# Second layer of a two-layer mixture: second-product matmuls issued in turn with first-product matmuls, and large tiles moved to one address phase

## The chip, the core and the metric

One core of one Trainium2 chip. The metric is the device time of one execution in microseconds, here the median of three runs.

## What is computed

Attention with a local window and some global keys over q, k, v (2 x 8 heads x 768 x 64) gives x, 1536 tokens by 512. A first layer follows, then a second layer of eight experts with a gate that is normalised over rows and columns in turn:

```python
x = x @ w_in                      # 512 -> 2048
g = h * (1.0 / (1.0 + np.exp(-h)))
x = g @ w_out                     # 2048 -> 512
...
for e in range(E):                # 8 experts
    h = np.maximum(x @ w1[e], 0.0)        # 512 -> 1024
    ye = h @ w2[e]                        # 1024 -> 512
    out += P[:, e:e + 1] * ye
```

All inputs and the output are float32.

## The kernel before, in words

Every float32 operand of a matmul is split into a high and a low part of the type that TensorE takes at full speed; a product is three matmuls (high by high, high by low, low by high) that add up in PSUM.

The program has three stages. Attention runs interleaved with the first layer (`step`, `emit_h`, `emit_y`), and the second layer (`layer2`) comes last. The change is in the second layer, and by the addresses of its tiles it touches the others.

The second layer works through 48 units. Unit u is one expert's half of the hidden columns (512 of 1024; 16 of these, counted by q) and one block of 512 tokens (tb, three of them). In a unit the first product x @ w1 is 512 x 512 x 512. It is made as seven products of 256-blocks with sums and differences of blocks (a fast 2 x 2 scheme, line 326 for the weights): `h_product(u, i)`, with i in 0, 5, 4, 6, 3, 1, 2 in this order. Each is 12 matmuls of 128 x 256, with the split weights `wc[i]` as the stationary and the split tokens `xc[tb][i]` as the moving operand. The results stand in PSUM banks: 0 and then 1 add up in the one bank "h", 5 and 6 in one of three banks "a", 4 and 2 in another, 3 in the third. DVE sums them (`h_sum`, lines 410, 476, 480), ACT applies the Relu and makes the high part (line 402), DVE the low part (line 403, `h_split`). The hidden values go into one of five pairs of tiles, room_hh / room_hl (three pairs), room_g and roomh / rooml.

The second product h @ w2 of a unit is made one unit later. `y_part(u - 1, k)`, k = 0..3, takes 128 hidden columns and issues 12 matmuls of 128 x 512: for each of four token tiles i three matmuls into bank `y[i]`, with hidden values as the stationary and w2 rows as the moving operand. After k = 3 the four banks are added to the output, weighted by the gate (`y_add`, line 440).

`window(u)` writes this order down by hand: product 0, 5, part 0, product 4, part 1, products 6 and 3, part 2, product 1, part 3, product 2. Parts are whole blocks of 12 matmuls, and so are products. A scheduler that looks at priorities then places each engine's instructions, so some move a little. In windows where new weights are due, `w_combine(i)` after a product and `w_split(k)` after a part make the next split weights with ACT and POOL (lines 342, 343).

Tiles lie in pools that grow from the left of a partition (xp, hid, wf, ring and the constants) and in pools on its right (the late one, gp, with wc0 to wc2, roomh, rooml and the tokens xc of the first two blocks). In the names of rows, xc_0xh, xc_1xh, xc_0xl and xc_1xl are the tokens of the third block, which lie on the left, plain xc those of the first two, on the right. wx0 and wx1 are weights on the left. Small tiles at the head of the pools set where the large ones begin: those on the left at 32 bytes past a multiple of 256, those on the right at 96 past.

Of the kernel before, what the change touches and what calls it, by code (L numbers as in the profile page):

```python
# [8 lines left out]
F32 = mybir.dt.float32  # L9
# [11 lines left out]
P = 128  # L21
# [16 lines left out]
HB = TB // 2  # L38
ORDER = 0, 5, 4, 6, 3, 1, 2
TINY = 1.125 * 2.0**-15  # L40

# [5 lines left out]
class Kernel:  # L47
# [29 lines left out]
    def setup(self, const, pre):  # L77
        nc = self.nc
# [28 lines left out]
        nc.vector.scalar_tensor_tensor(flag, self.ng, float(G), fl[:, 1:2], op0=ALU.is_le, op1=ALU.mult)  # L107
        self.flag = flag
        for _ in self.att_turn(0, const):
            pass  # L110
# [262 lines left out]
    def h_product(self, u, i):  # L373

        nc = self.nc
# [8 lines left out]
        for f in range(2):  # L384
            fs = slice(f * P, (f + 1) * P)
            for k in range(2):
                for a, b in ((ah, bh), (ah, bl), (al, bh)):
# [4 lines left out]
                    n += 1  # L392
        return ps

# [18 lines left out]
    def y_part(self, u, k, tiles=range(4)):  # L413
# [4 lines left out]
        for i in tiles:  # L418
# [3 lines left out]
            for j, (a, b) in enumerate(((hh, wh), (hh, wl), (hl, wh))):  # L422
                nc.tensor.matmul(  # L423
                    self.y[i], a, b, start=k == 0 and j == 0, stop=k == 3 and j == 2, skip_group_check=True
                )

    def y_add(self, u, i):
# [18 lines left out]
    def window(self, u, side):  # L446

        nc, n_units = self.nc, self.E * self.NH * self.NB
        q, tb = divmod(u, self.NB)
        y = iter(range(4)) if u else iter(())  # L450

# [3 lines left out]

        def second():
            k = next(y, None)
            if k is not None:
                self.y_part(u - 1, k)
                if u % self.NB == 0:  # L460
                    self.w_split((2, 3, 0, 1)[k])

        def first(i):
            ps = self.h_product(u, i)
            if more:
                self.w_combine(i)
            next(side, None)
            return ps

# [4 lines left out]
        b2 = first(5)  # L474
        second()
        nc.vector.tensor_tensor(u2, s1, b2, op=ALU.add)  # L476
        b3 = first(4)
        second()
        first(6)
        nc.vector.tensor_tensor(u3, s1, b2, op=ALU.add)  # L480
        b4 = first(3)
        hq[1, 1] = self.h_sum(u3, b3, ALU.add)
        hq[1, 0] = self.h_sum(u3, b4, ALU.subtract)
        second()
        first(1)
        hq[0, 0] = self.h_split(b1)
        second()
        if u:
# [11 lines left out]
    def layer2(self):  # L500
# [4 lines left out]
        for i in range(4):  # L505
            for k in range(4):
                self.y_part(n_units - 1, k, (i,))
            self.y_add(n_units - 1, i)
# [455 lines left out]
    def rest(self):  # L964

        yield from self.x_combine(self.NB - 1)
# [183 lines left out]
```

## Time and profile before

| | |
|---|---|
| runs | 1441.61, 1444.14, 1444.32 us, median 1444.14 |
| profiled execution | 1444.39 us |
| its span, first to last instruction | 1442.6 us |
| mean granted TensorE clock | 0.989 |
| TensorE matmuls busy | 1413.3 us (98% of the span), 8552 |
| weight loads busy | 1232.1 us (85%) |
| VectorE (DVE), ScalarE (ACT), GpSimd (POOL) busy | 739.9, 487.2, 553.6 us |

The busy time of TensorE is the time in which at least one matmul is recorded. Matmuls overlap in the records, so the mean duration of one (280 ns for 256 columns) is longer than the time from one start to the next. The chain that ended last follows the work back from the end: where an engine waited for nobody, it goes to the instruction before on the same engine.

### The profile page before, as it was taken

The numbers are of one execution on the slowest core, as the hardware profiler recorded it, in microseconds if no ns is written. First come the engines' busy times: TensorE is split into PE (matmuls) and PEld (weight loads), VectorE is DVE, ScalarE is ACT, GpSimd is POOL, SyncE is SP. The second block draws the span as 40 slices with busy tenths as digits, with TensorE's granted clock in tenths as the row PEclk, the third lists the DMA queues.
The fourth block names the chain that finished last, engine by engine and source line by source line (L and its number), as shares of the span: only waits on it lengthen the run. The fifth ranks groups of instructions, "written<-read, shape, count | busy, mean of one in ns | idle before, by whom it ended". The sixth has DMA issues, their size and how long they took to land.

```text
span 1442.6 us, 21250 instructions
## 1 busy us (share of the span) xinstructions
PE 1413.3 (98%) x8552; PEld 1232.1 (85%) x8552; DVE 739.9 (51%) x1298; ACT 487.2 (34%) x949; POOL 553.6 (38%) x489
## 2 busy tenths in 40 slices
PE   8998999999999999999999999999999999999998
PEld 6776687778888989999998999899899899989997
DVE  8899545456353556544354354435444443544443
ACT  6665545555352422222232221223222132322220
POOL 5677755444470423314142331414224141422210
PEclk8899999999999999999999999999999999999999
DMA  9685442222230201011010101102010110201001
GB/s 257 178 245 186 154 121 73 74 74 88 88 103 1 59 1 59 16 44 41 19 50 10 59 16 44 44 16 57 3 59 22 38 45 15 59 0 45 1 28 63
DMA packets 75292, 92.18 MB, mean 64 GB/s; under 512 B 30640, under 2 KB 49072, under 8 KB 75184
## 3 DMA queue, kind: packets, MB, share of 16 engines
q1 hardware_dynamic: 72880, 82.34, 19.2%
q10 hardware_dynamic: 2304, 8.39, 1.5%
q8 instruction: 69, 1.13, 0.3%
q14 instruction: 39, 0.32, 0.1%
HBM read 79.19 MB, written 11.53 MB: 63 GB/s over the span
## 4 chain that ended last, share of the span: by engine, by line
PE 89%; DVE 8%; issue 1%; ACT 1%; POOL 0%; DMA 0%; DVEq 0%; ACTq 0%; SPq 0%; POOLq 0%
PE y L423 37%; PE h L388 32%; PE y L276 7%; PE h L237 3%; PE h L238 3%; PE h L239 3%; PE a_s L726 2%; DVE wf L201 1%; DVE wf L203 1%; DVE wf L199 1%; DVE wf L205 1%; PE a_o L783 1%; PE a_f L764 1%; DVE s L735 1%; DVE st L744 0%
## 5 line engine op out<-in xcount | busy, mean ns | idle before, releaser
L480 DVE TENSOR_TENSOR tabs<-tabs,h 128x512 f32<-128x512 f32 x48 | 33.0, 687 | 333.9 <-PE h L388 333.9
L343 POOL TENSOR_TENSOR wc0l<-wf,wc0h 128x512 fp32r<-128x512 f32 x16 | 21.2, 1323 | 340.3 <-ACT wc0h L342 340.3
L440 DVE SCALAR_TENSOR_TENSOR x<-y,gate,x 128x512 f32<-128x512 f32 x168 | 115.5, 742 | 18.3 <-PE y L423 18.3
L343 POOL TENSOR_TENSOR wx1l<-wf,wx1h 128x512 fp32r<-128x512 f32 x64 | 89.9, 1405 | 79.7 <-ACT wx1h L342 79.5
L402 ACT ACTIVATE room_hh<-tabs 128x512 fp32r<-128x512 f32 x87 | 54.2, 629 | 190.9 <-DVE tabs L410 188.5
L410 DVE TENSOR_TENSOR tabs<-tabs,h 128x512 f32<-128x512 f32 x144 | 98.8, 687 | 19.0 <-PE h L388 16.8
L343 POOL TENSOR_TENSOR wx0l<-wf,wx0h 128x512 fp32r<-128x512 f32 x48 | 62.1, 1293 | 90.3 <-ACT wx0h L342 90.3
L388 PE MATMUL h<-xc,wx1h 128*128 128x256 f32 x512 | 93.4, 280 | 1.7 <-DVE tabs L410 1.7
L388 PE MATMUL h<-xc,wx0h 128*128 128x256 f32 x512 | 93.4, 280 | 0.6 <-DVE tabs L476 0.6
L423 PE MATMUL y<-wx1h,room_hh 128*128 128x512 f32 x232 | 91.2, 393 | 0.0
L423 PE MATMUL y<-wx0h,room_hh 128*128 128x512 f32 x232 | 91.2, 393 | 0.0
L423 PE MATMUL y<-wx0l,room_hh 128*128 128x512 f32 x232 | 90.8, 391 | 0.0
L423 PE MATMUL y<-wx1l,room_hh 128*128 128x512 f32 x232 | 90.8, 391 | 0.0
L423 PE MATMUL y<-wx0h,room_hl 128*128 128x512 f32 x232 | 90.7, 391 | 0.0
L423 PE MATMUL y<-wx1h,room_hl 128*128 128x512 f32 x232 | 90.7, 391 | 0.0
L403 DVE SCALAR_TENSOR_TENSOR room_hl<-tabs,room_hh 128x512 fp32r<-128x512 f32 x87 | 77.6, 898 | 25.5 <-ACT room_hh L402 24.2
L342 ACT ACTIVATE wx1h<-wf 128x512 fp32r<-128x512 f32 x64 | 40.4, 632 | 141.8 <-PE y L423 84.2
L388 PEld LDWEIGHTS h<-xc,wx0h 128*128 128x128 f32 x512 | 82.6, 188 | 5.8 <-DVE tabs L476 0.8
L221 POOL TENSOR_TENSOR w1l<-wf,w1h 128x512 fp32r<-128x512 f32 x48 | 67.0, 1395 | 50.9 <-ACT w1h L220 44.6
L388 PEld LDWEIGHTS h<-xc,wx1h 128*128 128x128 f32 x512 | 80.4, 188 | 4.4 <-DVE tabs L410 1.9
L221 POOL TENSOR_TENSOR w0l<-wf,w0h 128x512 fp32r<-128x512 f32 x48 | 67.0, 1397 | 42.0 <-ACT w0h L220 40.2
L276 PE MATMUL y<-hh,w1h 128*128 128x512 f32 (+1 forms) x208 | 83.0, 399 | 0.0
(270 smaller groups left out, 4143.3 us busy)
## 6 DMA issues: line engine op xcount, KB each, us to landing
wf<-in_moe_w_dram SPq DMA_DIRECT2D x64, 512.0 KB, 3.7
wf<-w SPq DMA_DIRECT2D x32, 512.0 KB, 3.3
ra<-in_moe_w_in_dram SPq DMA_DIRECT2D x16, 512.0 KB, 6.0
rb<-in_moe_w_out_dram SPq DMA_DIRECT2D x16, 512.0 KB, 5.3
w<-wf ACTq DMA_DIRECT2D x16, 512.0 KB, 4.3
vw<-in_v_dram SPq DMA_DIRECT2D x8, 448.0 KB, 4.5
qr<-in_q_dram SPq DMA_DIRECT2D x12, 256.0 KB, 5.8
kr<-in_k_dram SPq DMA_DIRECT2D x12, 256.0 KB, 6.0
```

Source lines behind the costliest of these rows:

```text
L221: nc.gpsimd.tensor_tensor(lo, src, f32(hi), op=ALU.subtract)
L237: nc.tensor.matmul(ps, ah, bh, start=i == 0, stop=False)
L238: nc.tensor.matmul(ps, ah, bl, start=False, stop=False)
L239: nc.tensor.matmul(ps, al, bh, start=False, stop=i == last)
L276: nc.tensor.matmul(self.y[i][:, cols], a, b, start=begin and j == 0, stop=f == self.NF1 - 1 and j == 2, skip_group_check=True,)
L343: self.nc.gpsimd.tensor_tensor(dst[1], src, f32(dst[0]), op=ALU.subtract)
L388: nc.tensor.matmul(ps[:, f * HB:(f + 1) * HB], a[:, k, fs], b[:, k, :], start=first and n == 0, stop=n == 11, skip_group_check=True,)
L402: self.nc.scalar.activation(hi, src, AF.Relu)
L403: self.nc.vector.scalar_tensor_tensor(lo, src, 0.0, f32(hi), op0=ALU.max, op1=ALU.subtract)
L410: self.nc.vector.tensor_tensor(c, a, b, op=op)
L423: nc.tensor.matmul(self.y[i], a, b, start=k == 0 and j == 0, stop=k == 3 and j == 2, skip_group_check=True)
L440: nc.vector.scalar_tensor_tensor(acc, self.y[i], self.gate[:, t, e:e + 1], acc, op0=ALU.mult, op1=ALU.add)
```

## The change

In `window`, parts are no longer called as blocks. `h_product` and `y_part` became generators that give way after each matmul, and `first(i, k)` issues one matmul of product i, then one of part k, twelve times. Product 4 goes with part 0, 6 with part 1, 3 with part 2, 1 with part 3; products 0, 5 and 2 stand alone. The last unit's parts, after the loop, stay blocks. Two pads that nothing reads are allocated: 224 bytes at the head of the left side (in `setup`) and 96 bytes on the right (in `rest`). With them every large tile that a matmul of the two layers reads begins at a multiple of 256 bytes.

```diff
+PAD_L, PAD_R = 224, 96
...
         self.flag = flag
+
+        const.tile([P, PAD_L // 4], F32, tag="pad", name="pad")
...
     def h_product(self, u, i):
...
                     n += 1
-        return ps
+                    yield
...
     def y_part(self, u, k, tiles=range(4)):
...
+                yield
...
-        y = iter(range(4)) if u else iter(())
...
-        def second():
-            k = next(y, None)
-            if k is not None:
-                self.y_part(u - 1, k)
-                if u % self.NB == 0:
-                    self.w_split((2, 3, 0, 1)[k])
-
-        def first(i):
-            ps = self.h_product(u, i)
+        def first(i, k=None):
+
+            second = self.y_part(u - 1, k) if u and k is not None else iter(())
+            for _ in self.h_product(u, i):
+                next(second, None)
+            if u and k is not None and tb == 0:
+                self.w_split((2, 3, 0, 1)[k])
             if more:
                 self.w_combine(i)
             next(side, None)
-            return ps
+            return self.hb[{0: 0, 1: 0, 5: 1, 6: 1, 4: 2, 2: 2, 3: 3}[i]]
...
         b2 = first(5)
-        second()
         nc.vector.tensor_tensor(u2, s1, b2, op=ALU.add)
-        b3 = first(4)
-        second()
-        first(6)
+        b3 = first(4, 0)
+        first(6, 1)
         nc.vector.tensor_tensor(u3, s1, b2, op=ALU.add)
-        b4 = first(3)
+        b4 = first(3, 2)
         hq[1, 1] = self.h_sum(u3, b3, ALU.add)
         hq[1, 0] = self.h_sum(u3, b4, ALU.subtract)
-        second()
-        first(1)
+        first(1, 3)
         hq[0, 0] = self.h_split(b1)
-        second()
...
     def rest(self):
-
+        self.gp.tile([P, PAD_R // 4], F32, tag="pad", name="pad")
```

What the scheduler makes of it, on TensorE where product 4 of unit 25 meets part 0 of unit 24. Before (names: h_25_4 is the bank of that product, y_24_3 that of token tile 3):

```order
L423 MATMUL y_24_2_8621<-wx0h_4209,room_hl_4218 128x512
L423 MATMUL y_24_3_8625<-wx0h_4209,room_hh_4215 128x512
L423 MATMUL y_24_3_8625<-wx0l_4210,room_hh_4215 128x512
L423 MATMUL y_24_3_8625<-wx0h_4209,room_hl_4218 128x512
L388 MATMUL h_25_4_8630<-xc_4_3710,wc2h 128x256
L388 MATMUL h_25_4_8630<-xc_11_3717,wc2h 128x256
L388 MATMUL h_25_4_8630<-xc_4_3710,wc2l 128x256
```

The whole part stands ahead of the whole product. In the changed program, the head of the same product, with the last rows of product 5 before it:

```order
L391 MATMUL h_25_5_8602<-xc_12_3719,wc1h 128x256
L391 MATMUL h_25_5_8602<-xc_5_3712,wc1l 128x256
L391 MATMUL h_25_4_8616<-xc_4_3711,wc2h 128x256
L426 MATMUL y_24_0_8618<-wx0h_4210,room_g_4220 128x512
L391 MATMUL h_25_4_8616<-xc_11_3718,wc2h 128x256
L426 MATMUL y_24_0_8618<-wx0l_4211,room_g_4220 128x512
L391 MATMUL h_25_4_8616<-xc_4_3711,wc2l 128x256
L426 MATMUL y_24_0_8618<-wx0h_4210,room_g_4221 128x512
```

Each matmul of the product is now followed by one of the part.

The second place is TensorE at the head of a window, unit 25 after product 2 of unit 24. Before:

```order
L388 MATMUL h_24_4_8466<-xc_9_3447,wx1h_4203 128x256
L388 MATMUL h_24_4_8466<-xc_2_3440,wx1l_4204 128x256
L388 MATMUL h_25_0_8586<-xc_0_3706,wc0h 128x256
L388 MATMUL h_25_0_8586<-xc_7_3713,wc0h 128x256
L388 MATMUL h_25_0_8586<-xc_0_3706,wc0l 128x256
```

In the changed program:

```order
L391 MATMUL h_24_4_8450<-xc_9_3448,wx1h_4204 128x256
L391 MATMUL h_24_4_8450<-xc_2_3441,wx1l_4205 128x256
L391 MATMUL h_25_5_8602<-xc_5_3712,wc1h 128x256
L391 MATMUL h_25_5_8602<-xc_12_3719,wc1h 128x256
L391 MATMUL h_25_0_8588<-xc_0_3707,wc0h 128x256
L391 MATMUL h_25_0_8588<-xc_7_3714,wc0h 128x256
```

Two matmuls of product 5 now stand ahead of product 0, the one that writes bank "h".

The third place is DVE at the end of window 22. Before (x_0 is the output of a token block, y_21_0 to y_21_3 the four banks of the second product, h_22_0 the bank "h", h_22_4 the bank of products 4 and 2):

```order
L403 SCALAR_TENSOR_TENSOR room_hl_4217<-h_22_0_8078,room_hh_4214 128x512
L440 SCALAR_TENSOR_TENSOR x_0_2317<-y_21_0_8105,gate,x_0_2317 128x512
L440 SCALAR_TENSOR_TENSOR x_0_2317<-y_21_1_8109,gate,x_0_2317 128x512
L440 SCALAR_TENSOR_TENSOR x_0_2317<-y_21_2_8113,gate,x_0_2317 128x512
L440 SCALAR_TENSOR_TENSOR x_0_2317<-y_21_3_8117,gate,x_0_2317 128x512
L410 TENSOR_TENSOR tabs<-tabs,h_22_4_8122 128x512
```

In the changed program:

```order
L444 SCALAR_TENSOR_TENSOR x_0_2318<-y_21_0_8110,gate,x_0_2318 128x512
L406 SCALAR_TENSOR_TENSOR room_hl_4217<-tabs,room_hh_4214 128x512
L444 SCALAR_TENSOR_TENSOR x_0_2318<-y_21_1_8117,gate,x_0_2318 128x512
L444 SCALAR_TENSOR_TENSOR x_0_2318<-y_21_2_8124,gate,x_0_2318 128x512
L444 SCALAR_TENSOR_TENSOR x_0_2318<-y_21_3_8131,gate,x_0_2318 128x512
L406 SCALAR_TENSOR_TENSOR room_hl_4218<-h_22_0_8080,room_hh_4215 128x512
L413 TENSOR_TENSOR tabs<-tabs,h_22_4_8108 128x512
```

The read of bank "h" (line 403, now 406) moved from ahead of the four additions to behind them. (Lines 388, 402, 403, 410, 423 and 440 of the kernel before are 391, 405, 406, 413, 426 and 444 of the changed one.)

## Rows read from the trace of the kernel before

**Rows 1.** The page, parts 1 and 4: busy time, and the chain by engine.
```profile
PE 1413.3 (98%) x8552; PEld 1232.1 (85%) x8552; DVE 739.9 (51%) x1298; ACT 487.2 (34%) x949; POOL 553.6 (38%) x489
...
PE 89%; DVE 8%; issue 1%; ACT 1%; POOL 0%; DMA 0%; DVEq 0%; ACTq 0%; SPq 0%; POOLq 0%
```

**Rows 2.** Second layer: PE, PEld, DVE, ACT, POOL busy (count), clock, DMA share, GB/s.
```profile
420.90:1437.20 1016.30, 1013.03 (x6377) 913.68 (x6375) 475.33 (x704) 255.80 (x427) 302.43 (x227) 1.00 0.11 34
```

**Rows 3.** The same stretch, line 388 alone and line 423 alone: PE, PEld, clock, DMA.
```profile
420.90:1437.20 1016.30, 509.32 (x4032) 503.67 (x4031) 1.00 0.11 34
...
420.90:1437.20 1016.30, 561.98 (x2304) 419.77 (x2304) 1.00 0.11 34
```

**Rows 4.** Chain of waits, one window: start us, length us, what.
```profile
941.97 4.29 PE h L388 x36
946.25 2.75 PE y L423 x12
949.00 1.43 PE h L388 x12
950.43 2.75 PE y L423 x12
953.18 2.83 PE h L388 x24
956.01 2.79 PE y L423 x12
958.80 1.42 PE h L388 x12
960.22 2.78 PE y L423 x12
```

**Rows 5.** TensorE's timeline, four stretches, first and last row: start, length, what.
```profile
902.82 0.28 PE L388 MATMUL h<-xc_0xl,wc1l 128*128 128x256 f32 x1
...
903.95 0.40 PE L423 MATMUL y<-wx0h,room_hh 128*128 128x512 f32 x1
...
911.05 0.28 PE L388 MATMUL h<-xc_1xl,wx0h 128*128 128x256 f32 x1
...
912.37 0.28 PE L388 MATMUL h<-xc_0xh,wx1h 128*128 128x256 f32 x1
...
1020.27 0.39 PE L423 MATMUL y<-wx0h,room_hh 128*128 128x512 f32 x1
...
1021.63 0.40 PE L388 MATMUL h<-xc,wx0h 128*128 128x256 f32 x2
...
1010.43 0.40 PE L423 MATMUL y<-wx0h,roomh 128*128 128x512 f32 x1
...
1011.84 0.40 PE L388 MATMUL h<-xc,wc2h 128*128 128x256 f32 x2
```

**Rows 6.** The end: chain piece of the last 48 y; timeline of the last matmul and addition.
```profile
1426.12 11.06 PE y L423 x48
...
1436.77 0.40 PE L423 MATMUL y<-wx1h,room_hl 128*128 128x512 f32 x1
1437.20 0.75 DVE L440 SCALAR_TENSOR_TENSOR x<-y,gate,x 128x512 f32<-128x512 f32 x1 [2.04 <-PE y L423]
```

**Rows 7.** Weight loads (page; tile lg: ns min/median/max), and lg's matmuls in the timeline.
```profile
L388 PEld LDWEIGHTS h<-xc,wx0h 128*128 128x128 f32 x512 | 82.6, 188 | 5.8 <-DVE tabs L476 0.8
...
L534 PEld LDWEIGHTS lg<-xc,wg x40: 93/94/96, 344.1 to 373.8; 128*16 128x16 f32 x40
...
344.34 1.88 PE L534 MATMUL lg<-xc,wg 128*16 128x256 f32 x15
```

**Rows 8.** DVE's timeline after product 1 of one window: start, length, what.
```profile
1023.93 0.69 DVE L403 SCALAR_TENSOR_TENSOR room_hl<-h,room_hh 128x512 fp32r<-128x512 f32 x1 [2.71 <-ACT room_hh L402]
1024.54 2.71 DVE L440 SCALAR_TENSOR_TENSOR x<-y,gate,x 128x512 f32<-128x512 f32 x4
```

**Rows 9.** Groups of the page: line 403 where it reads SBUF.
```profile
L403 DVE SCALAR_TENSOR_TENSOR room_hl<-tabs,room_hh 128x512 fp32r<-128x512 f32 x87 | 77.6, 898 | 25.5 <-ACT room_hh L402 24.2
```

More of the change, by code (lines that the diff above doesn't have):

```diff
@@ L446, in window @@
     def window(self, u, side):
-        nc, n_units = self.nc, self.E * self.NH * self.NB
+        nc = self.nc
         q, tb = divmod(u, self.NB)
-        y = iter(range(4)) if u else iter(())
         more = tb == self.NB - 1 and q + 1 < self.E * self.NH
@@ L506, in layer2 @@
             for k in range(4):
-                self.y_part(n_units - 1, k, (i,))
+                for _ in self.y_part(n_units - 1, k, (i,)):
+                    pass
             self.y_add(n_units - 1, i)
```

## The prediction

> **What bounds the kernel now.** I read the page first, then the busy time of the last stage, then the chain of waits inside it, then single steps of TensorE in the timeline. The page gives TensorE 1413.3 us of matmuls in a span of 1442.6 us, and the chain that ended last is 89% TensorE [rows 1]. The change lives in the second layer, from 420.9 to 1437.2 us: 1016.3 us at a granted clock of 1.00, that is 2.4 GHz, with TensorE busy for 1013.0 of them, so idle for 3.3 [rows 2]. There line 388 issues all 4032 matmuls of the first products ("h", 256 columns) and line 423 all 2304 of the second ("y", 512 columns) [rows 3]. The stage is a stream of matmuls, and its length is their number times the time from one start to the next, which I call a step. Busy times don't give steps, because records overlap; the chain does, since it counts each matmul from the end of the one before. One whole window there holds 9.97 us of 84 h (118.7 ns) and 11.07 us of 48 y (230.6 ns) [rows 4]. Check: 4032 x 118.7 + 2304 x 230.6 = 478.6 + 531.3 = 1009.9 us, with the idle time within 3 us of the stage.
>
> At 2.4 GHz 256 columns are 106.7 ns and 512 are 213.3 ns, so each h carries 12.0 ns and each y 17.3 ns that are not columns: 48.4 + 39.9 = 88 us in all. Only these 88 us, and new waits, can move. They aren't constant. Ten steps of 128x256 with xc_0xl and wc1 took 1.13 us (113 ns), eleven with xc_0xl and wx0 took 1.32 us (120 ns); six y with room_hh and room_hl took 1.36 us (226.7 ns), six with roomh and rooml 1.41 us (235 ns) [rows 5]. Shape, clock and neighbours are alike, so the difference must come from where the tiles lie. As the program is laid out, tiles of the left side begin 32 bytes past a multiple of 256, those of the right side 96 past.
>
> **The change, term by term.**
>
> *Taking turns.* No matmul is added or removed. Products 4, 6, 3 and 1 of 47 units are issued one h, one y, 12 + 12. If a step depended on its neighbour's kind, blocks of different length would show it. Blocks of 12 h take 1.42 and 1.43 us, of 24 2.83, of 36 4.29: 118 to 119 ns whatever the length; blocks of 12 y take 2.75 to 2.79, which is 229 to 233 ns, and the last 48 in one piece 11.06, which is 230.4 [rows 4, 6]. So I take 0. A block of 12 could hide 5 ns per change of kind from me, so the bounds are 96 x 47 changes x 5 ns, 22 us either way.
> One might expect more because of the weight load: one of 128 columns is recorded with 188 ns, one of 16 columns with 94 [rows 7], so 128 columns cost some 107 ns, as long as an h streams, and a y gives it twice that time. But 15 matmuls of 256 columns with those 16-column loads still take 14 steps in 1.88 - 0.28 us, 114 ns each [rows 7]. A shorter load barely shortens the step; a longer cover for the load shouldn't either.
>
> *One phase.* The pads of 224 and 96 bytes bring every large tile to a multiple of 256. The trace never shows that place: every operand of these two lines begins 32 bytes past a multiple of 64. Bounds: at the best all 88 us go; at the worst every step becomes the dearest seen, 120 and 235 ns, +5.2 +10.1 = +15 us. The rows point both ways. For h equal places are dear (xc_0xl with wx0, both at 32: 120) and unequal ones cheap (xc_0xl at 32 with wc1 at 96: 113); for y equal ones are cheap (226.7) and unequal ones, roomh and rooml at 96, dear (235) [rows 5]. What speaks for a gain is the ratio of the cheap steps: 113/106.7 and 226.7/213.3 are both 17/16. One column's time is added for every 16 columns, that is for every 64 bytes streamed, which is what a stream would pay whose pieces of 64 bytes each straddle a boundary. With that removed the steps should at least come down to the cheap ones. I take the nearest rows: 114 ns for h (113 to 114 [rows 5, 7]) and 228 for y, a little over 226.7 since most y now stand between two h: (118.7 - 114) x 4032 = 19.0 us and (230.6 - 228) x 2304 = 6.0 us, together -25.0 us.
> The Trainium skill ("TensorE: Matmul & The Clock Gate", Part 2, step 1) says that TensorE reads the moving operand and the weights through two independent ports, so that loading weights takes nothing from a running matmul. By it no placing of weights against moving tiles could matter, and this term would be 0; rows 5 show 113 against 120 ns, so here the measurement decides against it.
>
> *A new wait.* Product 0 of the next unit writes the one bank "h" that product 1 of this unit fills, so it waits until ACT and DVE have read it (lines 402 and 403). Before, a block of 12 y stood between, 2.8 us of slack. Now DVE makes the four additions of line 440 first, as the order of the change shows. The last addition starts 0.43 us after the last y starts, 0.03 after that y's record ends [rows 6]; the next instruction of DVE follows 0.68 us later (four in 2.71) and takes 0.69 [rows 8]. So the bank is free 1.80 us after that y starts, and 0.03 more for the signal. TensorE meanwhile has that y, 12 h of product 2 and 2 of product 5, which the scheduler put in front: 0.23 + 14 x 0.1187 = 1.89 us, or 1.83 with h at 114 ns. Nothing to spare, and nothing waited if all is on time. Line 403 has a mean of 898 ns where it reads SBUF [rows 9], against 0.69 us where it reads the bank; were DVE late by that 0.21 us every time, 46 windows would cost 9.7 us. Between 0 and 9.7 I take 3 us, nearer to on time.
>
> *What costs nothing.* Splitting the next weights (lines 342, 343) is issued at the end of the same products; ACT and POOL are busy for 255.8 and 302.4 us of the stage's 1016.3 [rows 2], and the queue of DMA issues is in the same order. If that cover went, product 5 of the next unit would wait for its weights. The four additions need to free their banks before product 4 of the next unit, 36 h or 4.2 us after the last y, and are done in 1.1.
>
> **The sum.** The profiled execution took 1444.39 us, 0.25 us above the median of 1444.14. 1444.4 + 0 - 25.0 + 3 = 1422.4, say **1422 us**.
>
> **The rivals.** A difference under 0.2% (2.9 us) can't be told from none here; all chances use that bound.
>
> 1. *Neither part does anything.* The steps stay as they are, and the wait stays near 0 to 3: **1446 us** at the middle. For: blocks of every length have the same step. Against: steps do depend on place. Chance 0.18.
>
> 2. *Slower: equal places are the dear case for h.* The weight load and the stream hit the same part of SBUF together, as xc_0xl with wx0 does. 4032 x (120 - 118.7) = +5.2 us, y at 229.5 -2.5, the wait +3 to +9.7: **1450 to 1457 us**. It decides as soon as h steps stand above 118.7 ns. For: the equal-place rows of h [rows 5]. Against: those were also off the 64-byte grid, and no row shows them on it. Chance 0.30.
>
> 3. *The whole extra column per 16 goes.* Steps of 109 and 217 ns: (118.7 - 109) x 4032 + (230.6 - 217) x 2304 = 39.1 + 31.3 = 70 us less, the wait grows to 5: **1379 us**, and something less again if the first layer's matmuls gain alike. For: the ratio 17/16. Against: nothing in the trace runs at such a step, and the extra may be the chip's own. Chance 0.12.
> The Trainium skill (same page, "Back-to-back issue gap") gives N/2.4 + 2.5 ns for a warm stream, 109 and 216 ns; by it the result would be an estimate of some 1377 us. No step of this trace is that short.
>
> **How the numbers follow.** Forecast 0.40, rivals 0.18, 0.30 and 0.12. The forecast spreads over 1405 to 1439 as h lands between 111 and 117 ns. Faster: 0.40 + 0.12 = 0.52; same 0.18; slower 0.30. A range of 80% leaves out most of rival 3 and the upper end of rival 2: 1390 to 1455 us.
>
> **What would show it.** Right: in the chain, 12 h plus 12 y in 4.10 us or less (4.18 to 4.22 now as two blocks), blocks of h alone at 114 ns, and under 0.1 us of idle before product 0 in each window. Rival 1: all blocks as now. Rival 2: h alone at 120 and the pair at 4.2 or more. Rival 3: pairs at 3.95. The forecast is wrong if blocks of h still show 118 ns or more, or if TensorE's waits on DVE exceed 10 us.

## The result, and the profile after

The changed kernel takes **1460.82 us** (median of 4 runs, 1458.88 to 1462.03) against 1444.16 (four runs of the kernel before): 1.0115 times as long, 95% interval 1.0102 to 1.0129, so 16.7 us slower. The forecast was 1422 with a range of 1390 to 1455: the sign is wrong, and the time lies above the range. The profiled execution took 1458.88 us with a span of 1457.1.

The page, parts 1 and 4, the lines that answer to [rows 1]:

```profile
PE 1429.9 (98%) x8552; PEld 1237.0 (85%) x8552; DVE 735.2 (50%) x1298; ACT 488.0 (33%) x949; POOL 546.1 (37%) x489
...
PE 89%; DVE 7%; POOL 1%; ACT 1%; issue 1%; DMA 0%; ACTq 0%; SPq 0%; DVEq 0%; POOLq 0%
```

TensorE has the same 8552 matmuls and is busy 16.6 us longer. Its weight loads grew by 4.8 us and ACT by 0.8; DVE and POOL are busy for less time than before. The second layer alone, whole and then by its two matmul lines (h is now line 391, y line 426), the columns of [rows 2, 3]:

```profile
418.90:1452.00 1033.10, 1029.83 (x6377) 919.28 (x6375) 472.83 (x705) 256.88 (x426) 293.38 (x227) 1.00 0.11 33
...
418.90:1452.00 1033.10, 851.93 (x4032) 644.53 (x4031) 1.00 0.11 33
...
418.90:1452.00 1033.10, 810.05 (x2304) 432.92 (x2304) 1.00 0.11 33
```

The layer went from 1016.3 us [rows 2] to 1033.1, at the same granted clock of 1.00, and TensorE is idle for 3.3 us in both. So the loss is in the steps of one stream; a short wait shows there as a longer step and not as idle time, since the records overlap. (The busy times of the two lines overlap each other here and can't be added.) The chain of waits shows one unit of work:

```profile
905.00 0.23 PE y L426
905.23 4.51 PE h L391 x37
909.75 0.23 PE y L426
...
926.36 0.23 PE y L426
926.59 4.53 PE h L391 x37
931.12 0.23 PE y L426
```

A unit is 36 h in one piece, then 48 pairs of one h and one y (the 37th h of a piece is that of the first pair). From one piece of 37 to the next it is 21.36 us; before, from the 36 h at 941.97 to the end of the last 12 y at 963.00, 21.03 [rows 4]. Inside the pairs, TensorE's timeline (the first rows, and the 22nd pair after):

```profile
930.96 0.40 PE L426 MATMUL y<-wx0h,roomh 128*128 128x512 f32 x1
931.19 0.28 PE L391 MATMUL h<-xc,wc2h 128*128 128x256 f32 x1
931.31 0.40 PE L426 MATMUL y<-wx0l,roomh 128*128 128x512 f32 x1
931.55 0.28 PE L391 MATMUL h<-xc,wc2l 128*128 128x256 f32 x1
...
938.73 0.40 PE L426 MATMUL y<-wx1l,room_g 128*128 128x512 f32 x1
```

22 pairs take 7.77 us, 353.2 ns a pair; twelve would be 4.24 us, where the forecast wanted 4.10. Averaged over the 2248 y that stand between two h, from start to start, a y takes 236.2 ns and an h 117.0.

To price the parts I averaged all steps of the second layer by kind and by neighbours, leaving out those lengthened by a wait. All y went from a mean of 230.3 to 236.0: 2304 x 5.7 = 13.1 us. All h stayed, 118.25 and 118.1: those between y fell to 117.0 and those among h rose to 119.7, -0.6 us in sum. The waits at product 0 are 4.1 us more. Together 16.6 of the 16.7 that the layer has grown.

The waits, in the timelines of TensorE and its weight loads, and of DVE:

```profile
926.20 0.40 PE L426 MATMUL y<-wx1h,room_hl 128*128 128x512 f32 x1
...
927.86 0.40 PE L391 MATMUL h<-xc,wc1h 128*128 128x256 f32 x2
928.10 0.30 PEld L391 LDWEIGHTS h<-xc,wc0h 128*128 128x128 f32 x2
928.13 0.47 PE L391 MATMUL h<-xc,wc0h 128*128 128x256 f32 x2
928.44 0.28 PE L391 MATMUL h<-xc,wc0l 128*128 128x256 f32 x1
```

```profile
926.63 0.75 DVE L444 SCALAR_TENSOR_TENSOR x<-y,gate,x 128x512 f32<-128x512 f32 x1 [0.31 <-PE y L426]
927.30 0.68 DVE L406 SCALAR_TENSOR_TENSOR room_hl<-h,room_hh 128x512 fp32r<-128x512 f32 x1
```

This answers to [rows 6, 8]. The last y starts at 926.20, the last addition 0.43 us later, and the bank is read until 927.98, 1.78 us after that y where 1.80 was forecast. Two h of product 5 take 0.27 us instead of 0.24, and the first two of product 0 take 0.31: a gap of 0.03 and a first step some 0.07 too long. The long step stands in 46 units, a gap in 40. The first load of weights for product 0 shows why: it starts at 928.10, 0.12 us after DVE's read ends, where a load otherwise starts 2 to 5 ns after the start of the matmul ahead of its own. Over the trace most of these 46 loads start 115 ns after DVE's read, and behind 41 of them the next load is late by some 75 ns, which is the long first step.

### The profile page after: what moved, and what is told of

The parts are those of the page before. It is cut to its first block, busy times and chain, and to the rows that moved or that the text cites. A ratio compares the mean times of both kernels' runs of the same rounds, so it can differ in the third digit from the quotient of the medians.

```text
span 1457.1 us, 21265 instructions
## 1 busy us (share of the span) xinstructions
PE 1429.9 (98%) x8552; PEld 1237.0 (85%) x8552; DVE 735.2 (50%) x1298; ACT 488.0 (33%) x949; POOL 546.1 (37%) x489
## 3 DMA queue, kind: packets, MB, share of 16 engines
q10 hardware_dynamic: 2304, 8.39, 1.5%
## 4 chain that ended last, share of the span: by engine, by line
PE 89%; DVE 7%; POOL 1%; ACT 1%; issue 1%; DMA 0%; ACTq 0%; SPq 0%; DVEq 0%; POOLq 0%
PE y L426 37%; PE h L391 32%; PE y L279 8%; PE h L240 3%; PE h L242 2%; PE h L241 2%; PE a_s L724 2%; DVE wf L204 1%; DVE wf L206 1%; PE a_o L781 1%; DVE wf L202 1%; PE a_f L762 1%; DVE wf L208 1%; POOL s L745 1%; DVE s L733 1%
## 5 line engine op out<-in xcount | busy, mean ns | idle before, releaser
L444 DVE SCALAR_TENSOR_TENSOR x<-y,gate,x 128x512 f32<-128x512 f32 x168 | 124.6, 748 | 47.2 <-PE y L426 44.1
L391 PE MATMUL h<-xc,wx0h 128*128 128x256 f32 x512 | 141.8, 280 | 0.6 <-DVE tabs L476 0.6
L346 POOL TENSOR_TENSOR wx1l<-wf,wx1h 128x512 fp32r<-128x512 f32 x64 | 82.9, 1295 | 121.6 <-ACT wx1h L345 121.5
L391 PE MATMUL h<-xc,wx1h 128*128 128x256 f32 x512 | 117.9, 281 | 1.4 <-DVE tabs L413 1.4
L391 PEld LDWEIGHTS h<-xc,wx0h 128*128 128x128 f32 x512 | 96.2, 189 | 0.8 <-DVE tabs L476 0.8
L406 DVE SCALAR_TENSOR_TENSOR room_hl<-tabs,room_hh 128x512 fp32r<-128x512 f32 x87 | 74.0, 851 | 41.9 <-ACT room_hh L405 41.9
L391 PEld LDWEIGHTS h<-xc,wx1h 128*128 128x128 f32 x512 | 89.9, 190 | 3.2 <-DVE tabs L413 1.6
L345 ACT ACTIVATE wx0h<-wf 128x512 fp32r<-128x512 f32 x48 | 30.3, 632 | 150.0 <-PE y L426 109.8
```

The source lines that it names most:

```text
L345: self.nc.scalar.activation(dst[0], src, AF.Copy)
L346: self.nc.gpsimd.tensor_tensor(dst[1], src, f32(dst[0]), op=ALU.subtract)
L391: nc.tensor.matmul(ps[:, f * HB:(f + 1) * HB], a[:, k, fs], b[:, k, :], start=first and n == 0, stop=n == 11, skip_group_check=True,)
L406: self.nc.vector.scalar_tensor_tensor(lo, src, 0.0, f32(hi), op0=ALU.max, op1=ALU.subtract)
L444: nc.vector.scalar_tensor_tensor(acc, self.y[i], self.gate[:, t, e:e + 1], acc, op0=ALU.mult, op1=ALU.add)
```

## The experiments

Eighteen kernels; run 15 stands ahead of 13 and 14, which build on it. "Stage" is the time from the first h to the start of the last y; "in a run" means with two neighbours of its own kind. A y or h "at a change" stands first behind the other kind. All steps are ns from start to start. A dash means that the kernel has no whole y. A mean can mix two rates: the 36 h and the 12 h of run 16, and the h of runs 5 and 9 ahead of a wait and behind it.

| run | what | median us | ratio to before [95%] | stage us | h in a run | h at a change | y in a run | y at a change |
|---|---|---|---|---|---|---|---|---|
| - | before | 1444.2 | 1 | 1015.9 | 118.3 | 117.0 | 230.2 | 234.5 |
| - | the change | 1460.8 | 1.0115 [1.0102, 1.0129] | 1032.6 | 119.7 | 117.0 | 227.2 | 236.2 |
| 1 | turns alone | 1451.1 | 1.0045 [1.0032, 1.0057] | 1023.5 | 118.3 | 116.4 | 230.0 | 233.3 |
| 2 | pads alone | 1446.1 | 1.0008 [1.0000, 1.0017] | 1017.9 | 119.9 | 113.3 | 228.7 | 233.4 |
| 3 | blocks, xc at 192 | 1435.4 | 0.9935 [0.9922, 0.9948] | 1005.5 | 117.6 | 117.5 | 226.8 | 226.8 |
| 4 | twos, pads | 1454.4 | 1.0062 [1.0048, 1.0077] | 1025.6 | 120.0 | 114.6 | 227.1 | 232.9 |
| 5 | turns, xc at 192 | 1452.2 | 1.0055 [1.0041, 1.0068] | 1021.9 | 117.0 | 117.1 | 227.6 | 232.8 |
| 6 | blocks, xc at 128 | 1451.1 | 1.0052 [1.0038, 1.0065] | 1021.5 | 119.8 | 116.6 | 230.3 | 232.5 |
| 7 | the change, 5 ahead of 0 | 1457.3 | 1.0095 [1.0080, 1.0110] | 1028.6 | 119.9 | 117.0 | 227.2 | 236.3 |
| 8 | run 3, all 32 further | 1436.3 | 0.9951 [0.9937, 0.9964] | 1005.5 | 117.7 | 117.5 | 226.8 | 226.8 |
| 9 | run 3, turns of one kind | 1448.5 | 1.0031 [1.0020, 1.0042] | 1018.7 | 117.0 | 117.5 | 227.0 | 229.4 |
| 10 | blocks, xc at 224 | 1443.7 | 0.9997 [0.9987, 1.0007] | 1013.7 | 118.2 | 120.8 | 229.1 | 233.9 |
| 11 | blocks, xc at 64 | 1440.9 | 0.9980 [0.9971, 0.9989] | 1012.8 | 117.8 | 118.3 | 228.9 | 240.5 |
| 12 | blocks, xc at 160 | 1444.1 | 0.9996 [0.9987, 1.0005] | 1012.8 | 118.9 | 116.7 | 227.9 | 231.3 |
| 15 | run 5, 5 ahead of 0 | 1446.6 | 1.0016 [1.0006, 1.0025] | 1017.1 | 117.4 | 117.0 | 226.7 | 232.9 |
| 13 | run 15 in twos | 1440.1 | 0.9971 [0.9962, 0.9981] | 1010.4 | 113.7 | 119.1 | 226.9 | 232.5 |
| 14 | run 15, y in halves | 1448.6 | 1.0032 [1.0019, 1.0045] | 1019.0 | 113.8 | 117.8 | - | - |
| 16 | run 3, one last y in halves | 1430.6 | 0.9900 [0.9884, 0.9917] | 1000.3 | 116.0 | 118.3 | 227.0 | 228.0 |
| 17 | run 3, all last y in halves | 1426.9 | 0.9866 [0.9847, 0.9886] | 996.0 | 114.1 | 120.7 | 227.7 | 231.5 |
| 18 | run 3, one nudge a block | 1427.3 | 0.9879 [0.9862, 0.9895] | 997.1 | 113.7 | 118.7 | 228.0 | 232.5 |

The first layer ends at 418.7 to 424.1 us in these traces, also among kernels with the same places; so I read steps and the stage from the traces, and times from the medians. The pads move tiles of the first layer too: with xc at 192 that end lies at 420.7 to 424.1 in nine traces, at one phase at 418.7 to 421.8 in four, so the medians gain a little less than the stage.

**Run 1, turns alone.** The change without its two pad tiles:

```diff
-        const.tile([P, PAD_L // 4], F32, tag="pad", name="pad")
-        self.gp.tile([P, PAD_R // 4], F32, tag="pad", name="pad")
```

> The change without its two pads: one h, one y in turn, every tile where it lay before (32 and 96 bytes past a multiple of 256). Theory A (the kind of the matmul ahead sets the step: a y that follows an h is dear, an h that follows a y a little cheap; in the changed kernel 236.2 and 117.0 ns against 230.6 and 118.7 before): y between two h at 234 to 237 ns, h between two y at 115 to 118, some 2250 pairs dearer by 3 to 5 ns, 7 to 11 us, and 3 us of waits for bank h: 1453 to 1458 us. Rival B (the equal places are what costs): steps stay at 118 to 119 and 230 to 231, only the 3 us of waits: 1445 to 1449 us.

Measured 1451.1, under the range of theory A and above that of B. A pair takes 233.3 + 116.4 = 349.7 against 118.25 + 230.3 = 348.55 before: 2250 x 1.1 = 2.6 us. The waits for bank h, 5.5 us in this trace, are the larger part. Taking turns at the old places costs little by itself.

**Run 2, pads alone.** The kernel before with the two pads of the change:

```diff
+PAD_L, PAD_R = 224, 96
+        const.tile([P, PAD_L // 4], F32, tag="pad", name="pad")
+        self.gp.tile([P, PAD_R // 4], F32, tag="pad", name="pad")
```

> The two pads alone, matmuls in blocks of 12 as before. Theory A: h among h at 119.7 to 120.2 ns (4032 x 1.3 = +5 us), y among y at 227 to 228 (2304 x -3 = -7 us), no new wait: 1440 to 1445 us. Rival B: the equal places cost all of the rise but the 3 us of waits: 1455 to 1459 us, with y at 234 ns or more inside its blocks.

Measured 1446.1, +1.4 us (by the interval 0 to 2.5), a little above the range of A; B is out. The chain of waits, and the weight loads of h (tile, count, ns as min/median/max):

```profile
952.18 2.87 PE h L390 x24
955.05 2.75 PE y L425 x12
957.80 1.43 PE h L390 x12
...
961.98 4.31 PE h L390 x36
```

```profile
L390 PEld LDWEIGHTS h<-xc,wx0h x496: 187/192/192, 442.3 to 1400.5; 128*128 128x128 f32 x166
```

h takes 4.31 / 36 = 119.7 everywhere, and 192 ns is recorded for most of its weight loads, 188 before [rows 7]. In a block of y, steps 1 to 5 behind an h average 233.4, 235.6, 228.5, 232.4 and 230.8; from the sixth on they are 226.7. So at one phase a run settles, at 13.3 ns above the columns for **both** kinds: 106.7 + 13.3 = 120 and 213.3 + 13.3 = 226.7. (A settled y is 226.7 in every kernel with pads and whole y; a settled h is not always 120, as the later runs show.) And it takes a y five steps to settle after an h: 27 ns in sum, of which the first h of the next block (113.3) gives 6.7 back. Run 1 and run 2 together give +8 us and the change, which is both, +16.7. My reading, which no run tests by itself: in turns a y never gets as far as its sixth step, so it loses what a block gains at one phase.

**Run 3, blocks with xc 64 bytes short.** Run 2 with two pads more, so that weights and rooms lie at 0 and xc, the moving tiles of h, at 192 past a multiple of 256:

```diff
-PAD_L, PAD_R = 224, 96
+PAD_L, PAD_R, PAD_H, PAD_X = 160, 160, 64, 192
+            self.hp.tile([P, PAD_H // 4], F32, tag="pad", name="pad_h")
+            self.gp.tile([P, PAD_X // 4], F32, tag="pad_x", name="pad_x")
```

> Blocks as before, all weights and rooms on multiples of 256, but the moving tiles of h (xc) 64 bytes short of one. If the step hangs on the place of the moving tile against that of the weights (the rows of before have 113 ns where xc lay at 32 and wc at 96): h at 113 to 116 ns, y at 227 to 228, 4032 x -4 and 2304 x -3: 1419 to 1430 us. Rival: the 113 ns belong to those two tiles and not to the 64 bytes; h stays at 118 to 120: 1437 to 1445 us.

Measured 1435.4: 9.3 us faster than before, between the two ranges. The chain, and the same view of the weight loads:

```profile
951.00 2.83 PE h L390 x24
953.83 2.72 PE y L425 x12
956.55 1.41 PE h L390 x12
...
960.68 4.24 PE h L390 x36
```

```profile
L390 PEld LDWEIGHTS h<-xc,wx0h x496: 187/188/188, 447.4 to 1393.7; 128*128 128x128 f32 x166
L390 PEld LDWEIGHTS h<-xc,wx0l x248: 192/192/192, 447.8 to 1393.8; 128*128 128x128 f32 x124
```

h came down only to 117.6, but y sits at 226.7 from the first step on: 12 y in 2.72 us. Moving only the tiles of **h** took the settling away from the **y**. So the place of the tiles of one kind bears on how the next kind starts.

**Run 4, two h and two y.** The change with

```diff
-            for _ in self.h_product(u, i):
-                next(second, None)
+            for n, _ in enumerate(self.h_product(u, i)):
+                if n % 2:
+                    next(second, None)
+                    next(second, None)
```

> The change with its pads, but two h, then two y in turn. Theory A (the price is paid at each change from h to y): only every second y follows an h, 234 to 236 ns, the other 227 to 229; every second h follows a y, 114, the other 120. Half of the changes, so half of the price: 1447 to 1452 us. Rival A2 (any y that stands beside an h is dear, behind or ahead of it): both y at 234 to 237 and the time stays at 1458 to 1462. Rival B (places): stays at 1458 to 1462 too, with y at 234 or more also in the last 48 that stand in one piece.

Measured 1454.4, between the ranges. Both y are dear, 232.9 and 233.3, as A2 had it; but both h are cheap, 114.6 and 115.9, so a pair is 348.4, what blocks at these places take (119.9 + 228.7 = 348.6). What is left over run 2 is waiting: beyond the start of the stage, steps at and ahead of product 0 lost 8.3 us in this trace and 0.3 in run 2's.

**Run 5, turns with xc at 192.** The change with the four pads of run 3.

> The change (one h, one y in turn) at the places of the third run: weights and rooms on multiples of 256, xc 64 bytes short of one. So far blocks at one phase took 13.3 + 15.4 ns above the columns for an h and a y, turns there 10.3 + 22.9; blocks with xc 64 short 11.0 + 13.5. Theory P (taking turns is dear because of where xc lies against the weights and rooms): the extra of a pair falls from 33.2 to about 24.5 to 26, 2250 pairs x 8 ns, and h among h by 2.4 ns: 1437 to 1442 us, which is the third run's 1435 and 3 to 5 us of waits for bank h. Theory N (taking turns costs 4.5 ns a pair wherever the tiles lie): 28 to 30 ns a pair, 1446 to 1451 us.

Measured 1452.2, a miss just above N, and P is out. y between h takes 232.8 and h 117.1, 349.9 a pair, where run 3 has 344.4. Places that take the settling out of blocks leave turns 5.5 ns a pair dearer.

**Run 6, xc at 128, and run 8, everything 32 bytes further.** Run 3 with the pads below in run 6, and with 192, 128, 64, 192 in run 8:

```diff
-PAD_L, PAD_R, PAD_H, PAD_X = 160, 160, 64, 192
+PAD_L, PAD_R, PAD_H, PAD_X = 96, 224, 128, 128
```

> The third run with xc 128 bytes past a multiple of 256 instead of 192. If any unequal place of xc does, the same steps as there, h 117 to 118, y 226.8: 1433 to 1438 us. If it is the 64 bytes short that count, h back to 119 to 120 and the first y of a block to 233: 1442 to 1447 us.

> The third run with every large tile moved by 32 bytes: xc at 224, weights and rooms at 32 past a multiple of 256. If only the places against each other count: the same steps, 1433 to 1438 us. If a start on a multiple of 64 is what made y 226.8 (the kernel before lies at 32 and has 230.2): y back to 229 to 231, 2304 x 3 = +7 us, 1440 to 1445 us; h could fall to the 113 ns that xc at 32 and wc1 at 96 had before, 4032 x -4: 1418 to 1428 us.

Run 6 gives 1451.1: h back to 119.8, y to 230.3, worse than expected for either case. Run 8 gives 1436.3 with the steps of run 3 to 0.1 ns. So these steps are the same whether the tiles begin on a multiple of 64 or 32 bytes past one; what counted in runs 2, 3 and 6 is the place of xc against the rest.

**Runs 10, 11 and 12, other places of xc.** Run 3 with 192, 128, 32, 224 (xc at 224), 32, 32, 192, 64 (at 64), and 128, 192, 96, 160 (at 160) as the four pads.

> The third run with xc 32 bytes short of a multiple of 256 in place of 64. Known so far, h and first y of a block by the place of xc: 0: 119.9 and 233.4; 128: 119.8 and 232.5; 192: 117.6 and 226.8. If the step changes in pieces of 64 bytes: as 192 or as 0, 1433 to 1438 or 1444 to 1448 us. If it changes by bytes: between, 1438 to 1442.

> The third run with xc 64 bytes past a multiple of 256 in place of 192. In the kernel before, h with xc 64 past its weights had 117.8 ns (11.2 above the columns). If only the distance counts, ahead or behind alike: 1433 to 1439 us. If xc has to lie behind: h 120, y 229 to 230, 1443 to 1450 us.

> The third run with xc 96 bytes short of a multiple of 256 in place of 64. If the good places are a stretch around 192: 1433 to 1440 us. If 192 is one point: 1443 to 1451 us as at 0 and 128.

At 64 the h are as good as at 192, but the first y of a block costs 240.5, and the time, 1440.9, lies between the two ranges: a miss. At 224 and 160 the gain of run 3 is gone. 224 gives 1443.7, a miss by 0.3 us; 160 gives 1444.1, in the range of "192 is one point". Of six places 192 is by far the best (64 keeps 3 us of the gain), and the only one where y needs no steps to settle; I have no rule that would have named it.

**Run 7, product 5 ahead of product 0.** The change with

```diff
-        b1 = first(0)
-        nc.scalar.activation(s1, b1, AF.Copy)
         b2 = first(5)
+        b1 = first(0)
+        nc.scalar.activation(s1, b1, AF.Copy)
```

> The change with its pads; of the next unit product 5 is issued ahead of product 0, so that the bank h has 1.4 us more to be read. Theory: the 46 waits at product 0 (a gap of some 20 ns, and a first step of product 0 that is 75 ns too long, 4.4 us together in the trace of the change) go, the steps stay: 1455 to 1458 us. Rival: the long first step of product 0 isn't the bank's, and the time stays at 1459 to 1462.

Measured 1457.3, 3.5 us less than the change. The 37 h of a unit now take 4.43 us where they took 4.51 to 4.53, and all steps are those of the change:

```profile
904.32 4.43 PE h L391 x37
...
925.60 4.43 PE h L391 x37
```

The stage is 4.0 us shorter, and past the first units the late load is gone. So the waits were the bank's, and cost 3.5 to 4.1 us; the medians alone would not settle it, since the intervals of the two ratios overlap.

**Run 9, turns among one kind.** At the places of run 3, products 4 and 6 in turn, then 3 and 1, and the y parts two and two in turn:

```diff
+        def turn(a, b):
+            for _ in a:
+                next(b)
+            next(b, None)
...
+                turn(self.y_part(u - 1, k), self.y_part(u - 1, k + 1))
...
+                turn(self.h_product(u, i), self.h_product(u, j))
```

> Turns among matmuls of one kind, at the places of the third run: products 4 and 6 in turn, then 3 and 1 (24 h that change bank, weights and moving tile at each step), and the y parts two and two in turn (24 y that change their moving tile at each step); no h ever alternates with a y. Turns of h with y at these places took 117.1 and 232.8 ns, blocks 117.6 and 226.8. Theory K (the price is the mix of the two widths): h stays at 117 to 118, y at 226.8, the time at 1433 to 1438 us. Rival C (the price is the change of bank and tiles at each matmul): y up by 3 ns or more, or h by 2, 1441 us or more.

The steps are those of theory K, the time (1448.5) is not, and it would point to C if read alone:

```profile
952.52 5.46 PE y L426 x24
957.97 2.83 PE h L391 x24
960.80 5.44 PE y L426 x24
966.24 7.19 PE h L391 x60
```

24 h that change bank, weights and moving tile at each step take 2.83 us, 117.9 each, as 24 in order do in run 3; 24 y take 227 each. The time went into the last piece: 60 h would be 7.05 us and take 7.19, and over the stage, beyond its start, the steps at and ahead of product 0 lose 14.6 us, against 0.4 in the kernel before; product 1, issued later here, fills the bank that product 0 needs. So changing bank, weights or tiles among matmuls of one kind costs nothing; changing from h to y does.

The wait does one thing more. TensorE's timeline around one, product 5 and then product 0:

```profile
970.32 0.28 PE L391 MATMUL h<-xc_0xl,wc1h 128*128 128x256 f32 x1
970.54 0.39 PE L391 MATMUL h<-xc_0xh,wc0h 128*128 128x256 f32 x1
970.76 0.28 PE L391 MATMUL h<-xc_0xl,wc0h 128*128 128x256 f32 x1
...
973.15 0.28 PE L391 MATMUL h<-xc_0xl,wc1l 128*128 128x256 f32 x1
```

Two steps of 0.22 us, and then 21 steps take 2.39 us, 113.8 each. In 42 of 46 such pieces the h behind the wait have a mean under 115.5, those ahead of it 117.8. So a short wait, too, can leave the h behind it at a cheaper step, which runs 13, 14 and 16 to 18 reach without one. At one phase it did not: in the changed kernel the h behind the waits run at 119.5, those ahead at 119.9.

**Run 15, run 5 without the waits.** Run 5 with the edit of run 7.

> Turns of one h, one y at the places of the third run, product 5 of the next unit ahead of product 0, so without the waits for bank h: the price of taking turns by itself against the third run's blocks (1435 us). By the steps so far (117.1 + 232.8 against 117.6 + 226.8, 2250 pairs): +12 us, 1444 to 1449 us. If the waits hid nothing else, it lies 4 to 6 us under the fifth run's 1452.

Measured 1446.6, as expected: 11.2 us over run 3, which is 2250 pairs at 5.0 ns. This is the price of taking turns at places where blocks are cheap.

**Run 13, run 15 in twos, and run 14, run 15 with y in halves.** Run 13 adds the edit of run 4, run 14 this one:

```diff
+                for c in range(2):
+                    nc.tensor.matmul(
+                        self.y[i][:, c * HB:(c + 1) * HB], a, b[:, c * HB:(c + 1) * HB],
```

> As the run before, but two h, then two y. Theory K (the price belongs to a change between the widths 256 and 512): half the changes, half the price: 1438 to 1443 us. Rival (a y is dear as soon as h are mixed in at all): 1444 to 1449 us.

> As the run before the last (one h, one y in turn), but every y as two matmuls of 256 columns, so that all matmuls have one width while bank, weights and moving tile still change between kinds. Theory K: every step, of h and of both halves, at 117 to 118.5 ns; three of them 351 to 355 against 349.9 for h and whole y, the rest of the y too 234 to 237 for two halves: 1443 to 1457 us. Rival P (it is the pair of an h and a y that is dear, whatever their widths, by the tiles they read): the half ahead of an h or behind one stays 5 to 6 ns above the other, a pair 356 or more: 1458 us or more.

Run 13 gives 1440.1, in the range of K, though not as K has it: both y of a pair are dear (232.5 and 232.4). Run 14 gives 1448.6: h takes 117.8, the halves 117.5 and 118.1. With one width everywhere no step among the pairs stands out, whatever kind lies ahead. (A half has a weight load of its own, so width and columns per weight load change together here; no run parts them.) What I had not expected stands in the table: in the two kernels the h in a run take **113.7** and **113.8** ns. A piece of run 13:

```profile
963.33 4.32 PE h L391 x38
```

The tiles lie exactly where runs 3, 5 and 15 have 117 to 118.

**Runs 16, 17 and 18: what runs ahead of a block of h.** All on run 3. In 16 and 17 the last y of the last part, or of every part, is issued as two matmuls of 256 columns; in 18 the last two y of a block come after the first two h of the next product.

```diff
-                nc.tensor.matmul(
-                    self.y[i], a, b, start=k == 0 and j == 0, stop=k == 3 and j == 2, skip_group_check=True
-                )
+                for c in (slice(0, HB), slice(HB, TB)) if i == 3 and j == 2 else (slice(0, TB),):
+                    nc.tensor.matmul(
+                        self.y[i][:, c], a, b[:, c], start=k == 0 and j == 0,
+                        stop=k == 3 and j == 2 and c.stop == TB, skip_group_check=True,
+                    )
...
+                part = self.y_part(u - 1, k)
+                for _ in range(10):
+                    next(part)
+                held.append((part, k))
```

(the loop is that of run 17, with "and k == 3" run 16; the last four lines are the core of run 18, where the four additions to the output also come after product 2 in program order, since the last y do)

> The third run, but the last y of the last part of each unit is issued as two matmuls of 256 columns, just ahead of the 36 h that follow. In the 13th and 14th kernels those 36 h ran at 113.7 ns at the same places where the third run and the 15th have 117.5. Theory S (what ran last ahead of a block of h sets the step of the whole block): after two matmuls of 256 columns the 36 h run at 114, the next y pay some 15 ns, the extra matmul 13: 47 x (36 x 3.8 - 28) = -5 us, 1428 to 1432 us. Rival (the state comes from the long alternation, not from the last matmul): 36 h at 117.5, 1434 to 1438 us.

> As the run before, but the last y of all four parts in halves. Theory S: all h at 114 to 115, 4032 x 3.5 = 14 us less, 188 x (15 + 13) ns = 5 us more: 1424 to 1428 us. Rival: 117.5 and 188 x 13 ns more: 1436 to 1440 us.

> The third run, but the last two y of each block are issued after the first two h of the next product (10 y, 2 h, 2 y, 10 h), no matmul more. Theory S: from the state of the third run the two y could stay at 227 and the h at 117.5 (1434 to 1438 us), or the change tips the h to 113.7 for the rest of the block, 10 of 12 h and 34 of 36, while four y of a block pay 5 ns: 1425 to 1431 us. Rival (every change of width costs 5 ns): two changes more in each of 188 blocks, 1437 to 1440 us.

Measured 1430.6, 1426.9 and 1427.3, each inside a range of theory S (run 18 in that of its second case, where the h tip to 113.7). Run 16 has both cases in one unit; its chain:

```profile
954.00 2.73 PE y L426 x13
956.72 4.10 PE h L390 x36
960.82 2.73 PE y L426 x12
963.56 1.41 PE h L390 x12
```

Behind the 13 y, whose last two are the halves, 36 h take 4.10 us, 113.9 each; behind 12 whole y, 12 h take 1.41 us, 117.5 each. The weights and xc of both lie at the same places. Run 17, the same view and its weight loads:

```profile
951.63 1.38 PE h L390 x12
953.01 2.74 PE y L426 x13
955.75 4.10 PE h L390 x36
959.85 2.74 PE y L426 x13
```

```profile
L390 PEld LDWEIGHTS h<-xc,wx0h x496: 187/188/192, 447.5 to 1384.3; 128*128 128x128 f32 x166
L390 PEld LDWEIGHTS h<-xc,wx0l x248: 187/188/192, 447.8 to 1384.4; 128*128 128x128 f32 x124
```

All blocks of h are at 114 to 115 now, and the second line is 188 where run 3 had 192. 13 y with a matmul more take 2.74 us, 0.02 more than 12. Run 18 does it without one:

```profile
951.40 2.28 PE y L427 x10
953.69 0.24 PE h L390 x2
953.92 0.47 PE y L427 x2
954.39 3.86 PE h L390 x34
```

The two y behind the two h pay some 6 ns each, the 34 h that follow take 113.5 each, 4 ns less than in run 3. Both versions beat the kernel before by 17.6 to 17.9 us and the change by more than 33. Their intervals overlap, so neither beats the other.

## Why the prediction was wrong

**What bounds the kernel: right.** The stage is one stream, and its length is steps; but for DVE's read of bank "h" (the wait below) no other engine and no transfer showed up in the loss.

**Taking turns: the term of 0 was wrong.** It measures +2.6 us at the old places (run 1), about +11 at the new ones (the change without its waits, run 7, against run 2: 1457.3 - 1446.1), +11.2 at those of run 3 (run 15). The step that failed is "118 to 119 ns whatever the length ... So I take 0": the sum over a block can't show a price at its edge, since a first y that is dearer by 4 ns changes a block of 2.75 us by less than the 0.01 us to which the row is given. The steps at the edges were in the trace: the 185 y behind an h had a mean of 234.5 there, those inside 230.2, and the h behind a y 117.0 against 118.3. That is 3 ns a pair, some 7 us, and would have given the sign but not the size. I bounded the price at 5 ns a change, which holds (the pair, two changes, rose by 4.7), and took the middle of the bound. Nor are the two terms independent, as the sum had them: the same turns cost 2.6 us at the old places and 11 at the new ones.

**One phase: -25 was wrong, it is +1.4** (run 2, 0 to 2.5 by the interval). This is the larger error. The step that failed is "With that removed the steps should at least come down to the cheap ones", drawn from "113/106.7 and 226.7/213.3 are both 17/16 ... for every 64 bytes streamed". At one phase only y settles at its cheap step, 13.3 ns above the columns; h settles at its dear one, 13.3 as well, and not at the 6.7 of its cheap step. So the mean h became dearer by 1.4 and the mean y cheaper by 1.4. Run 8, 32 bytes further with the same steps, speaks against a boundary of 64 bytes. The ratio itself is not refuted: where h does reach its cheap step (113.4 to 113.8 in runs 13, 14, 17 and 18) it and the settled y of 226.7 are again both 17/16 of the columns to within 0.5 ns, and no block of 12 in twenty kernels lies more than 0.2 ns below that. The rows of h at equal places (120) against unequal ones (113) [rows 5] gave the right value, and the argument from the ratio overruled them. Nor was the 113 a matter of place alone, as runs 13 to 18 show. The steps that the forecast wanted, 114 and 228, are those of run 17 (114.4 and 228.1 over all h and whole y), which takes 1426.9 us; what brought them is the matmul ahead of each block, with xc at 192.

**The wait: +3 was right in kind and nearly in size.** 4.1 us in the trace, 3.5 by run 7. DVE's times came out to 0.02 us, so "nothing waited if all is on time" was wrong. Two things were missing. The signal was put at 0.03 us and took 0.12, and what waits is the weight load of product 0, which is due one step ahead of its matmul. And once that load was late, the next step took some 0.07 us more.

**What was costed at nothing** stayed there: past the first units, the trace has no stall but that at product 0.

**The rivals.** The side that came true was rival 2, at 0.30, and its mark stands in the trace: h alone at 120, twelve pairs above 4.2 us. But its mechanism, equal places as the dear case for h, is worth only the +1.4 of run 2; most of the loss is the price of taking turns, which no rival had, so its side came out by luck as much as by reason. It let y fall to 229.5; the y went to 236. Rival 3 is out: in twenty kernels no settled run of h has a mean under 113 ns, and none of y one under 226.5 (its mark of 3.95 us for twelve pairs should be 3.91 by its own steps, and the forecast's spread for h at 111 to 117 ns comes to 1410 to 1434 us; neither changes the outcome). The formula of the Trainium skill ("TensorE: Matmul & The Clock Gate", "Back-to-back issue gap"), 109 and 216 ns, is not reached in any of them; that section gives it for a matmul by itself and not, as the prediction put it, for a stream. The same section says that in a stream of weight loads and matmuls both set the spacing. The traces don't settle that: in run 2 most steps of h are 120.0 with loads of 192 ns, but in run 3 they are 117.5 with loads of 192 and 117.7 with loads of 187 or 188.

The Trainium skill's rule of two independent read ports (same page, Part 2, step 1) fares as it did in the prediction: run 3 moves xc by 64 bytes against the weights, and the median load of wx0h goes from 192 to 188 ns, the h step from 119.9 to 117.6. So places do matter here, and the measurement decides against the rule as the prediction drew on it; that loads take reads from a running matmul, no run shows by itself.

## What to carry to other kernels

Read steps from start to start and by neighbour, not as the mean of a block: a price at the edge of a block, and the steps that settle after it, are what an interleaving multiplies. A long run of one matmul shape is not at a fixed rate; what ran just ahead of it can decide the rate of all of it (36 h in run 16, 34 in run 18), so a cheap probe (split or swap one matmul at the edge) is worth more than an argument about places. Before equal placing is taken for good, move one operand alone by 64 bytes and look at both kinds of matmul.

## What the hardware did that I had not expected

One and the same stream of h, at the same places, ran at 113.7 or 117.5 ns for 36 matmuls on end, by what stood ahead of it (run 16); a wait ahead could do the same (run 9). The settled extra has one value for y, 13.3 ns, in every kernel with pads and whole y, and several for h: 13.3 (run 2), some 11 (run 3), 6.7 to 7.1 (runs 13, 14, 17, 18). Whether it is at bottom an amount per matmul or a share of the columns, these values leave open. And the place of h's moving tile decided whether the y behind it needed five steps to settle or none (runs 2 and 3).

What carries this state inside TensorE stays open. The records show only that a matmul's next weight load starts 2 to 5 ns after the matmul's start at every rate (behind a wait, some 75 ns later). The load's recorded length goes with the step in run 2 but not in run 3. Why 192 is the good place of xc, and whether a state under 113 for h or under 226.5 for y can be had, was not found out.
